# Two attention blocks in one kernel: its written-out instruction order is exchanged for another one

## The chip, the cores and the metric

The kernel runs on one core of one Trainium2 chip. A core has TensorE (PE, matmul), VectorE (DVE), ScalarE (ACT), GpSimd (POOL) and SyncE (SP); they run side by side and wait for one another by semaphores. Data moves between the device memory and the on-chip memory by 16 DMA engines, and transfers are issued by SP, POOL or ACT. The metric is the device time of the whole program in microseconds (us), median of several runs; lower is better. The profile is of one execution of its own.

## The reference

Two attention blocks, A and B, each with its own input and weights, S = 2048 rows, D = 640 columns, 32 heads of 20; their outputs stand side by side.

```python
def _A_ref(x, wqkv, wo):
    H = 32; Dh = D // H; W = 256
    q, k, v = split(x @ wqkv)                       # per head, [S, 20]
    scores = einsum("bhqd,bhkd->bhqk", q, k) * Dh ** -0.5
    scores = where((0 <= i - j) & (i - j < W), scores, -1e9)
    return merge(softmax(scores) @ v) @ wo

def _B_ref(x, wqkv, wo):
    q, k, v = split(x @ wqkv)
    phi = lambda t: where(t > 0, t + 1, exp(t)) + 1e-6
    kv = einsum("bhsd,bhse->bhde", phi(k), v);  z = sum_s phi(k)
    num = phi(q) @ kv;  den = phi(q) . z + 1e-6
    return merge(num / den) @ wo
```

A is softmax attention in a sliding window of 256 rows; B is linear attention, where the keys and values are summed once over all rows and then applied to every query.

## The kernel before

The two blocks are cut into 1,382 operations, numbered in the order in which the code makes them. Each is a closure that emits one or a few instructions on one engine: a chain of matmuls into one PSUM bank, an evacuation, a DMA. `Graph.op` notes what an operation reads and writes. No scheduler runs when the kernel is built. `Graph.run` replays a written-out string, `ORDER`, whose items are `number:engine`, for a matmul chain also the banks and how many of its matmuls are emitted here (`1264:P::1`), so that two chains can be interleaved. The order in which items stand on one engine is the order of that engine's queue[...]. `ORDER` was found by a search elsewhere; the `size=`, `count=`, `fix=` and `issue=` arguments of `dma(...)` only tell that search how long a transfer is, and emit nothing.

The work, with the lines of the profile:

- Block A's projections: queries and keys of eight groups of four heads (L433, five 128x512 matmuls each), values (L466, five 128x320). A tile has 32 rows for each of four heads, of which a head takes 20; the projection fills the other twelve with rows of the heads of groups 5, 6 and 7, which are carried to tiles of their own through device memory: relay writes `dqk<-QK` (L454), then three relay reads `QK<-dqk` (L461), 512 KB each, for groups 5, 6 and 7, once for each half of the rows.
- Scores, in 78 *units* of 512 columns, numbered 0 to 77: 16 to 32 small matmuls (L538) into the one four-bank PSUM tile U, then one exponential of all of it on ScalarE (L544, tile PT), then masks on VectorE (L573). Since there is one U, L538 of a unit waits for L544 of the unit before it. The units serve here as the clock of the order: "after unit 48" is a place in TensorE's queue.
- Probabilities times values (L644), per half of the rows and group of four heads, 16 operations in two parts each; the denominators go to memory and back three times (`RC<-ON`, `dr<-RD`, `RB<-dr`; L678, L680, L682), then a multiply (L689). Rows of groups 5 to 7 go back to the other groups' tiles through `do<-OS` (L692) and `OT<-do` or `QK<-do` (L698, L701). A's output projection is L710.
- Block B: keys (L746, with L737 to L739 for phi), their sums over the rows (L754, with the input loaded once more as XT, L752), z (L766), the product with the value weights (L796), that with the output weights (L810), then a small matrix to memory and back (L818 to L820). B's queries are L831, its denominators L838, its output again L710.

The loads that matter below, all issued by SyncE: B's value weights into the tile WV, 800 KB, L947, when A's values (L466) have all been made, for WV holds A's until then; B's query weights into WQ, 800 KB, L822, when A's last query chain (L433) is done; X tiles transposed on the way, five per 512 rows, 128 KB each (L391). At the start: four row blocks of A's input (L478), A's value weights in two halves (L876), A's query and key weights in pieces into R (L408).

Everything is in one program of about 8,900 TensorE instructions, a weight load and a matmul in turn. [...] they appear in the profile as DMA packets of kind "instruction".

Of the kernel before, what the change touches and what calls it, by code (L numbers as in the profile page):

```python
# [7 lines left out]
P = 128  # L8
# [7 lines left out]
2:G 10:S 0:A 4:S 5:P 6:A 7:S 8:P 9:A 11:P 12:A 17:S 54:P:0:5 58:P:1:2 13:S 55:A 14:P 15:A 58:P::3 1:S 32:D 31:A 28:S 62:P:2:5 71:P:3:3 72:P::2 73:A  # L16
66:P:0:5 63:D 59:D 16:S 68:P:2:3 69:P::2 67:A 23:S 52:P:1:1 56:P:3:5 52:P::4 29:S 64:P:0:5 70:A 22:S 37:D 120:P:2:3 121:P::2 27:S 26:S 57:A 122:A
176:P 60:P:3:5 30:S 74:P:2:3 65:D 75:P::2 53:A 77:P:0:3 35:D 18:S 61:D 177:A 25:S 39:D 94:P:1:4 84:P:3:5 19:S 33:A 76:D 78:P::2 24:S 36:D 21:S 20:S
34:A 94:P::1 95:D 41:S 575:S 180:P 82:P:2:3 80:P:1:5 82:P::2 79:D 149:G 44:S 179:D 96:P:0:3 181:A 81:D 86:P:1:2 97:P::2 98:D 86:P::3 83:D 183:P 3:G
85:A 99:P:3:3 111:P:0:3 87:A 184:A 100:P::2 102:P:1:1 185:D 49:S 92:P:2:3 42:S 101:A 38:A 186:P 187:A 92:P::2 93:D 105:P:3:3 106:P::1 102:P::1  # L20
106:P::1 102:P::1 46:S 43:S 90:P:2:1 103:P::2 90:P::3 147:S 104:D 107:A 189:P 182:D 112:P::2 88:P:3:5 45:S 407:P:1:5 150:G 148:G 113:D 108:P:0:1 188:D
90:P::1 108:P::1 190:A 89:A 204:P 408:A 178:D 91:D 108:P::1 144:S 51:S 191:D 409:D 410:D 48:S 411:P:3:1 146:G 109:P::1 411:P::1 109:P::1 123:P:2:3
411:P::3 110:D 399:P:1:5 205:A 207:P 124:P::1 132:P:0:1 124:P::1 132:P::2 412:A 133:P::2 50:S 40:D 400:A 208:A 413:D 401:D 402:D 586:S 155:G 414:D
403:P:1:5 211:P 125:A 47:S 134:D 404:A 192:P:30 405:D 212:A 209:D 795:S 406:D 206:D 152:G 135:P:2:3 136:P::2 419:P:1:5 467:S 153:G 137:D 210:D 420:A
421:D 422:D 215:P 216:A 427:P:2:1 193:P 195:D 427:P::3 154:G 213:D 194:D 423:P:1:5 145:G 214:D 464:S 427:P::1 117:P:0:1 428:A 196:G 466:S 231:P 429:D
117:P::2 463:S 114:P:3:3 217:D 115:P::2 118:P::2 151:S 430:D 424:A 425:D 443:P:2:5 218:D 232:A 119:A 116:D 234:D 161:S 426:D 235:P 233:D 160:G 157:G
219:P:30 138:P:1:3 139:P::2 444:A 445:D 446:D 459:P:2:5 197:D 236:A 140:A 237:D 238:P 415:P:1:1 220:P 415:P::4 465:S 460:A 461:D 239:A 416:A 462:D
221:D 222:D 435:P:2:5 417:D 241:P 439:P:3:5 126:P:0:1 418:D 431:P:1:5 198:G 158:S 436:A 437:D 438:D 451:P:2:5 223:G 240:D 242:A 244:P 432:A 433:D
434:D 126:P::2 127:P::2 485:P:1:5 440:A 468:S 199:G 452:A 469:S 453:D 454:D 477:P:2:5 201:S 441:D 442:D 243:D 200:G 245:A 129:P:3:2 259:P 129:P::1
202:G 128:A 472:S 471:S 130:P::2 141:P:0:3 224:D 225:G 478:A 479:D 470:S 480:D 486:A 142:P::2 487:D 447:P:2:5 131:D 488:D 260:A 162:S 163:S 143:A  # L30
262:P 246:D 172:S 455:P:3:5 493:P:1:5 448:A 156:G 203:D 263:A 169:S 164:G 166:G 226:S 449:D 450:D 229:G 456:A 247:P:02 227:G 266:P 170:G 265:D 457:D
458:D 481:P:3:5 494:A 495:D 496:D 473:P:1:5 228:S 167:G 264:D 267:A 270:P 537:S 261:D 540:S 268:D 482:A 483:D 484:D 248:P 269:D 497:P:3:5 474:A 475:D
271:A 159:S 476:D 501:P:1:1 286:P 249:D 273:D 501:P::4 171:S 272:D 230:D 250:A 274:P:02 498:A 287:A 499:D 502:A 539:S 290:P 291:A 251:G 500:D
513:P:3:5 503:D 173:S 541:S 538:S 504:D 289:D 489:P:1:5 490:A 252:D 253:S 293:P 275:P 491:D 492:D 505:P:1:5 514:A 294:A 515:D 516:D 529:P:3:5 276:D
277:D 296:P 569:P:0:4 561:P:2:5 174:S 569:P::1 165:G 506:A 507:D 530:A 508:D 531:D 532:D 546:S 517:P:1:5 297:A 295:D 573:P:3:5 299:P 570:A 278:S 562:D
518:A 300:A 519:D 565:P:2:5 520:D 566:A 547:P:0:3 548:P::2 549:A 665:P:1:2 279:D 256:G 288:D 314:P 665:P::1 254:S 292:D 315:A 666:P::2 301:D 298:D
255:S 667:A 257:G 574:D 544:S 258:D 521:P:2:5 542:S 668:P:0:3 280:S 669:P::2 522:A 168:G 317:P 318:A 670:D 523:D 524:D 302:P:31 553:P:0:3 543:S
554:P::2 319:D 533:P:2:5 555:A 545:S 321:P 534:A 535:D 536:D 686:P:0:3 282:S 687:P::2 320:D 303:P 304:D 567:P:2:5 283:G 568:D 322:A 325:P 323:D
509:P:3:5 671:P:2:3 672:P::2 316:D 324:D 305:A 688:A 326:A 328:D 677:P:1:2 342:P 281:G 510:A 674:P:0:3 673:A 284:G 511:D 285:D 327:D 306:S 175:S 343:A
556:P:2:3 557:P::2 558:A 675:P::2 677:P::1 512:D 346:P 329:P:32 307:D 308:S 312:G 347:A 344:D 309:S 678:P::2 676:D 550:P:0:3 717:G 679:D 551:P::2  # L40
311:S 310:S 552:A 348:D 349:P 706:G 350:A 680:P:1:3 681:P::2 576:P:0:4 682:D 330:P 331:A 332:D 351:D 352:P 353:A 525:P:1:5 703:G 577:P::4 578:P::4
563:P:3:5 701:G 354:D 355:P 333:G 526:A 356:A 732:S 527:D 528:D 1079:S 683:P:2:3 684:P::2 685:A 564:D 698:P:1:2 579:P::4 698:P::1 371:P 689:P:3:3
690:P::2 1080:S 345:D 313:D 739:S 699:P::2 357:D 704:G 719:S 580:A 718:G 372:A 358:P:20 374:P 334:D 702:S 335:S 700:A 1078:S 691:D 375:A 733:S
656:P:3:3 657:P::1 692:P:1:1 657:P::1 692:P::2 377:D 339:S 338:S 658:A 693:P::2 694:A 378:P 379:A 359:P 361:D 662:P:3:3 653:P:1:3 654:P::2 336:S
663:P::2 360:D 382:P 383:A 337:S 659:P:0:1 587:P:2:4 659:P::2 373:D 660:P::2 664:D 381:D 661:A 655:D 376:D 1082:S 581:P:3:4 340:D 384:D 385:D 362:S
738:S 828:P 829:A 380:D 582:P::4 363:D 583:P::4 584:P::4 722:G 386:P:10 585:D 831:D 832:P 588:P::4 833:A 712:G 571:P:3:3 589:P::4 590:P::4 591:D
571:P::2 714:G 721:S 836:P 572:D 734:S 387:P 707:S 837:A 649:P:2:3 647:P:3:5 649:P::2 713:G 389:D 650:D 341:S 709:G 388:A 637:P:0:5 648:D 639:P:1:5
716:G 840:P 364:S 643:P:2:2 559:P:3:1 643:P::1 559:P::1 643:P::1 559:P::2 640:D 643:P::1 559:P::1 839:D 638:A 644:D 711:G 597:S 736:S 598:P:0:1
603:P:1:4 598:P::3 834:D 841:A 843:P 735:S 710:S 599:P::4 604:P::4 600:P::4 844:A 835:D 605:P::4 1081:S 846:P 366:G 560:D 606:P::4 601:P::4 847:A
641:P:2:1 368:S 365:G 842:D 651:P:3:5 390:S 391:D 641:P::4 830:D 367:G 720:G 794:S 737:S 369:D 862:P 849:D 652:A 848:D 645:P:3:5 838:D 642:A 607:D  # L50
863:A 845:D 602:A 646:D 715:S 695:P:2:3 696:P::1 850:P:13 864:D 392:S 866:P 867:A 592:P:0:4 593:P::4 594:P::4 595:P::4 696:P::1 697:A 708:S 705:S
869:P 370:G 619:S 851:P 596:D 396:S 630:P:0 395:S 620:P:2:4 621:P::4 622:P::1 865:D 852:D 393:G 870:A 872:P 873:A 622:P::2 625:P:1:4 626:P::4 627:P::4
628:P::2 394:G 397:D 871:D 853:D 875:P 631:D 628:P::1 1194:S 874:D 622:P::1 876:A 878:D 608:S 628:P::1 398:S 724:G 629:D 623:P::4 609:P:3:4 610:P::4
624:A 611:P::1 868:D 891:P 611:P::1 614:P:0:4 854:G 855:D 615:P::4 892:A 611:P::2 877:D 612:P::4 613:A 729:S 793:S 616:P::2 894:P 895:A 616:P::2
617:P::4 749:G 879:P:21 632:P:3 745:S 633:D 748:S 747:S 740:G 742:S 618:A 746:S 897:P 799:P:0:10 796:P:3:10 797:P::10 750:G 744:G 880:P 800:D 893:D
751:G 898:A 900:P 901:A 741:S 743:G 759:P:0:4 798:D 882:D 754:P:3:2 856:G 759:P::1 754:P::1 811:P:1 754:P::1 881:D 812:A 760:D 817:P:2 754:P::1
823:P:0 824:A 792:S 904:P 905:A 805:P:1 726:G 857:G 807:P:0 755:D 818:D 815:P:3 1136:S 896:D 1083:P:2:3 1084:P::2 1085:A 920:P 921:A 806:D 903:D 902:D
821:P:1 822:A 808:D 816:D 634:S 899:D 752:P:0:5 858:S 1093:P:3:3 883:S 1086:D 1087:D 923:P 907:D 859:S 753:A 924:A 860:S 906:D 1094:P::2 1139:S 1095:A
861:D 884:D 803:P:2 908:P:10 804:D 813:P:2 814:D 926:P 927:A 1088:P:2:3 909:P 1089:P::2 1135:S 930:P 1137:S 1096:D 1097:D 635:S 1103:P:3:3 1104:P::2
1090:A 910:D 911:D 1098:P:1:1 925:D 819:P:0 756:S 1091:D 1092:D 931:A 1098:P::1 934:P 1105:A 757:P:2:5 820:D 1098:P::1 1145:P:0:1 1099:P::2 885:S  # L60
727:S 730:S 1145:P::2 636:D 1138:S 728:S 935:A 723:G 889:S 951:P 1106:D 1107:D 801:P:3 932:D 933:D 912:S 1100:A 1146:P::2 952:A 887:S 758:D 762:P:2:5
# [133 lines left out]
def kernel(  # L195
# [11 lines left out]
    _, S, D = A_x.shape  # L207
# [6 lines left out]
    HALF = D // 2  # L214
# [606 lines left out]
    def b_wq(key, earliest):  # L821
        dma("SP", lambda q: q.dma_start(out=WQB[:], in_=wB[:, :, 0:D]), key, w=WQK0, earliest=earliest, tag="wqB", size=2100, count=640, fix=2.6)  # L822
# [176 lines left out]
```

## Time and profile before

| what | us |
|---|---|
| median of 7 runs | 270.54 |
| lowest, highest | 267.76, 272.08 |
| profiled execution, device time | 270.1 |
| its span, first to last instruction | 268.4 |
| TensorE busy | 249.9 |
| ScalarE busy | 209.6 |
| VectorE busy | 170.8 |
| GpSimd busy | 62.1 |

The page gives for each engine its busy time and share of the span, then the span in 40 slices of 6.7 us: a digit is a busy share in tenths, PEclk the TensorE clock that was granted, DMA the share of the 16 DMA engines. TensorE's ends are modelled, so a busy slice is not necessarily a dense one. In a timeline, a row is a start, a length, an engine and line, the tiles, the shape and the count; in brackets stands the idle time before it and what ended it. "issue" there means that nothing the profile shows was waited for.

### The profile page before, as it was taken

The numbers are of one execution on the slowest core, as the hardware profiler recorded it, in microseconds if no ns is written. First come the engines' busy times: TensorE is split into PE (matmuls) and PEld (weight loads), VectorE is DVE, ScalarE is ACT, GpSimd is POOL, SyncE is SP. The second block draws the span as 40 slices with busy tenths as digits, with TensorE's granted clock in tenths as the row PEclk, the third lists the DMA queues.
The fourth block names the chain that finished last, engine by engine and source line by source line (L and its number), as shares of the span: only waits on it lengthen the run. The fifth ranks groups of instructions, "written<-read, shape, count | busy, mean of one in ns | idle before, by whom it ended". The sixth has DMA issues, their size and how long they took to land.

```text
span 268.4 us, 10336 instructions
## 1 busy us (share of the span) xinstructions
PE 249.9 (93%) x4439; PEld 147.6 (55%) x4439; DVE 170.8 (64%) x391; ACT 209.6 (78%) x233; POOL 62.1 (23%) x146
## 2 busy tenths in 40 slices
PE   7899999998899999999999969888988999999992
PEld 3555455555555545456666646545545555577771
DVE  0244578778977675474645323989879996846550
ACT  4558888999998988977687863999989999963211
POOL 5006301245120114304020702011301123045300
PEclk9999999999999999999999995999999999999998
DMA  7989895498988335558987893589899356255652
GB/s 193 238 167 231 158 187 81 91 130 175 167 131 150 94 101 129 104 146 202 167 231 162 253 188 70 106 154 137 194 221 207 93 155 208 86 150 167 209 195 101
DMA packets 69877, 42.47 MB, mean 158 GB/s; under 512 B 56010, under 2 KB 64906, under 8 KB 69818
## 3 DMA queue, kind: packets, MB, share of 16 engines
q1 hardware_dynamic: 63014, 33.25, 55.4%
q0 software_dynamic: 4192, 8.23, 14.2%
q8 instruction: 35, 0.57, 1.0%
q10 hardware_dynamic: 2624, 0.33, 0.8%
q14 instruction: 12, 0.10, 0.1%
HBM read 24.29 MB, written 10.59 MB: 130 GB/s over the span
## 4 chain that ended last, share of the span: by engine, by line
PE 63%; SPq 12%; DMA 8%; ACT 7%; DVE 5%; issue 4%; DVEq 0%; ACTq 0%
PE F L433 12%; PE F L710 10%; PE F L754 9%; SPq L391 8%; PE U L538 7%; PE F L746 5%; PE F L644 5%; PE U L710 5%; PE F L831 5%; ACT PT L544 4%; DMA RC<-ON 4%; PE F L466 3%; DMA QK<-dqk 2%; SPq L408 2%; DMA X<-in_B_x_dram 1%
## 5 line engine op out<-in xcount | busy, mean ns | idle before, releaser
L544 ACT ACTIVATE PT<-U 128x2048 bf16<-128x2048 f32 x78 | 146.7, 1881 | 21.7 <-PE U L538 18.5
L573 DVE TENSOR_TENSOR PT<-PT,MK 128x512 bf16<-128x512 bf16 (+2 forms) x116 | 46.8, 424 | 16.5 <-ACT PT L544 16.2
L538 PE MATMUL U<-QK 20*64 20x128 bf16 (+4 forms) x1600 | 33.3, 252 | 6.1 <-ACT PT L544 4.8
L538 PEld LDWEIGHTS <-QK 20*64 20x64 bf16 x1600 | 16.2, 103 | 28.0 <-issue 26.5
L682 POOL DMA_DIRECT2D RB<-dr x31 | 15.7, 509 | 56.8 <-DMA dr<-RD 29.5
L454 POOL DMA_DIRECT2D dqk<-QK x36 | 18.8, 526 | 43.3 <-ACT QK L344 19.8
L746 PE MATMUL F<-W,X 128*128 128x320 bf16 x160 | 26.7, 300 | 1.2 <-DVE R L739 0.9
L831 PE MATMUL F<-X,WQ 128*128 128x512 bf16 x100 | 27.2, 384 | 0.2 <-DVE G L348 0.2
L739 DVE SCALAR_TENSOR_TENSOR R<-F,E 128x320 bf16<-128x320 f32 (+1 forms) x47 | 25.9, 553 | 1.3
L737 ACT ACTIVATE E<-F 128x320 bf16<-128x320 f32 (+1 forms) x52 | 25.1, 503 | 1.8 <-PE F L746 1.3
L754 PE MATMUL F<-R,XT 128*128 128x320 bf16 x160 | 24.6, 300 | 0.0
L644 PEld LDWEIGHTS <-V 64*32 64x32 bf16 x1556 | 19.1, 93 | 8.7 <-issue 6.9
L644 PE MATMUL F<-PT,V 64*32 64x320 bf16 (+4 forms) x1452 | 23.3, 251 | 0.0
L746 PEld LDWEIGHTS <-X 128*128 128x128 bf16 x160 | 14.8, 98 | 10.2 <-issue 2.4
L466 PE MATMUL F<-WV,X 128*128 128x320 bf16 x120 | 19.0, 300 | 1.1 <-DMA WV<-in_A_wqkv_dram 1.1
L433 PE MATMUL F<-X,WQ 128*128 128x512 bf16 x75 | 19.9, 380 | 0.0
L348 DVE COPY ON<-F 128x512 f32<-128x512 f32 x24 | 16.0, 687 | 5.5 <-PE F L644 5.5
L433 PE MATMUL F<-X,WK 128*128 128x512 bf16 x75 | 19.2, 380 | 0.1
L754 PEld LDWEIGHTS <-XT 128*128 128x128 bf16 x160 | 14.8, 98 | 7.5 <-issue 1.0
L738 DVE TENSOR_SCALAR E<-E 128x320 bf16<-128x320 bf16 (+1 forms) x52 | 13.6, 261 | 6.7 <-ACT E L737 6.7
L344 ACT CAST QK<-F 128x512 bf16<-128x512 f32 x23 | 13.4, 588 | 4.2 <-PE F L433 4.1
L348 DVE CAST V<-F 128x320 bf16<-128x320 f32 x20 | 9.6, 490 | 10.8 <-PE F L466 10.8
(104 smaller groups left out, 320.4 us busy)
## 6 DMA issues: line engine op xcount, KB each, us to landing
RB<-dr SPq DMA_DIRECT2D x33, 128.0 KB
RB<-dr POOLq DMA_DIRECT2D x31, 128.0 KB, 3.9
QK<-dqk SPq DMA_DIRECT2D x6, 512.0 KB
XT<-in_B_x_dram SPq DMA_DIRECT2D x5, 512.0 KB
out_dram<-G SPq DMA_DIRECT2D x10, 160.0 KB
out_dram<-ST SPq DMA_DIRECT2D x8, 160.0 KB
do<-OS SPq DMA_DIRECT2D x4, 256.0 KB
WV<-in_A_wqkv_dram SPq DMA_DIRECT2D x2, 400.0 KB
```

The lines of the kernel that those rows point to most:

```text
L348: nc.vector.tensor_copy(out=dst, in_=src)
L433: mms.append((mm_t(NX), xread(slot, k) + [("wqk", i, m)], lambda ps, k=k: nc.tensor.matmul(ps[:], lhsT=WQK[i][:, k, m * P : (m + 1) * P], ...
L466: mms = [(mm_t(HALF), (xread(slot, k) if slot or kb > 3 else [("xb", kb)]) + [("wv", hf)], lambda ps, k=k, hf=hf: nc.tensor.matmul(ps[:, 0 ...
L538: nc.tensor.matmul(upper.at(1)[0][64 * rho : 64 * rho + 64, j, cc : cc + w], lhsT=QK[g][32 * j : 32 * j + Dh, kc : kc + 64], rhs=QK[g][32 ...
L544: nc.scalar.activation(out=pt, in_=upper.at(1)[0][:], func=ACT.Exp, scale=scale)
L573: nc.vector.tensor_tensor(out=p, in0=p, in1=mk, op=ALU.mult)
L644: nc.tensor.matmul(FB[box[rg]][32 * j : 32 * j + 32, qc : qc + w], lhsT=V[kb % NV][64 * rho : 64 * rho + 64, HV * h : HV * h + 32], rhs=PT ...
L710: mms = [(mm_t(HALF), [lkeys(c)] if not isinstance(lkeys(c), list) else lkeys(c), lambda ps, c=c, hf=hf: nc.tensor.matmul(ps[:, 0:HALF], l ...
L739: ({"DVE": dve_ps(n)}, lambda e, ps: nc.vector.scalar_tensor_tensor(out=dst, in0=ps[:, 0:n], scalar=1.0 + 1e-6, in1=e1, op0=ALU.add, op1=A ...
L746: mms = [(mm_t(HALF), [("x", slot, k), ("w1",)], lambda ps, k=k, b=b, hf=hf: nc.tensor.matmul(ps[:, 0:HALF], lhsT=X[slot][:, k, b * P : (b ...
L754: mms = [(mm_t(HALF), [("r1", tb), ("xt", c % 2)], lambda ps, tb=tb, c=c, hf=hf: nc.tensor.matmul(ps[:, 0:HALF], lhsT=XT[:, c % 2, tb, :], ...
L831: mms = [(mm_t(NX), [("x", slot, k)] + WQK0, lambda ps, k=k, c=c: nc.tensor.matmul(ps[:], lhsT=WQB[:, k, :].rearrange("p (f c) -> p c f", ...
```

## The change

`ORDER` is replaced as a whole. The graph, its operations and their dependences stay: the same matmuls, evacuations and transfers are emitted, 1,474 items before and 1,529 after, since some matmul chains are cut into more pieces. Which evacuation runs on VectorE or ScalarE, and which of the free DMAs SyncE or GpSimd issues, is part of the string and changes with it (SyncE 225 items before and 215 after, GpSimd 107 and 117). Besides it, six `size=` arguments change: of the X loads (540 to 481), A's row blocks (1700 to 1280), XT (430 to 380), WQ for B (2100 to 1800), A's value weights (900 to 640) and WV for B (1850 to 1550). All lines of the code below the string move down by 4.

The numbers of the operations that the text speaks of: 866, 869, 872, 875, 891, 894, 897, 900 are units 43 to 50, 926 is unit 54; 608 is the load of XT; 398 `do<-OS`; 729, 730, 731 the relay reads `QK<-dqk`; 793 the load of WV, 792 that of WQ; 740 to 751 the twelve reads `OT<-do`; 796, 797, 799 the product L796; 16 and 17 the two halves of A's value weights; 22 and 23 two pieces of R.

```diff
 ORDER = """
-2:G 10:S 0:A 4:S 5:P 6:A 7:S 8:P 9:A 11:P 12:A 17:S 54:P:0:5 58:P:1:2 13:S 55:A 14:P 15:A 58:P::3 1:S 32:D 31:A 28:S 62:P:2:5 71:P:3:3 72:P::2 73:A
...
-869:P 370:G 619:S 851:P 596:D 396:S 630:P:0 395:S 620:P:2:4 621:P::4 622:P::1 865:D 852:D 393:G 870:A 872:P 873:A 622:P::2 625:P:1:4 626:P::4 627:P::4
-628:P::2 394:G 397:D 871:D 853:D 875:P 631:D 628:P::1 1194:S 874:D 622:P::1 876:A 878:D 608:S 628:P::1 398:S 724:G 629:D 623:P::4 609:P:3:4 610:P::4
-624:A 611:P::1 868:D 891:P 611:P::1 614:P:0:4 854:G 855:D 615:P::4 892:A 611:P::2 877:D 612:P::4 613:A 729:S 793:S 616:P::2 894:P 895:A 616:P::2
-617:P::4 749:G 879:P:21 632:P:3 745:S 633:D 748:S 747:S 740:G 742:S 618:A 746:S 897:P 799:P:0:10 796:P:3:10 797:P::10 750:G 744:G 880:P 800:D 893:D
-751:G 898:A 900:P 901:A 741:S 743:G 759:P:0:4 798:D 882:D 754:P:3:2 856:G 759:P::1 754:P::1 811:P:1 754:P::1 881:D 812:A 760:D 817:P:2 754:P::1
...
+2:G 0:A 4:S 10:S 7:S 17:S 13:S 23:S 3:G 1:S 22:S 5:P 26:S 8:P 6:A 9:D 11:P 16:S 54:P:0:5 28:S 12:A 32:D 14:P 55:A 62:P:1:2 15:A 58:P:2:5 24:S 30:S
...
+559:P::2 593:P::4 1194:S 594:P::4 644:A 864:D 595:P::2 560:A 866:P 640:A 595:P::2 867:A 850:P:20 608:S 695:P:1:3 793:S 696:P::2 596:A 869:P 697:D
+620:P:3:4 870:A 397:D 625:P:1:4 626:P::3 621:P::1 851:P 398:S 729:S 872:P 853:A 852:D 792:S 621:P::3 873:A 725:S 865:D 626:P::1 622:P::1 854:G
+627:P::3 871:D 868:D 622:P::3 630:P:0 874:D 875:P 631:A 614:P:2:4 876:A 609:P:0:4 750:S 742:G 610:P::4 751:S 746:G 611:P::3 744:S 627:P::1 878:D 741:S
+747:G 891:P 877:D 623:P::2 740:S 892:A 748:G 628:P::1 615:P::4 724:S 726:G 628:P::1 616:P::4 628:P::2 623:P::2 893:D 629:A 611:P::1 612:P::1 894:P
...
-    dma("SP", lambda q: q.dma_start(out=WV[:], in_=wB[:, :, 2 * D : 3 * D]), 118, w=[("wv", 0), ("wv", 1)], tag="wvB", size=1850, count=640, fix=2.6)
+    dma("SP", lambda q: q.dma_start(out=WV[:], in_=wB[:, :, 2 * D : 3 * D]), 118, w=[("wv", 0), ("wv", 1)], tag="wvB", size=1550, count=640, fix=2.6)
```

## The prediction, made before the changed kernel was run

> **What bounds the kernel now.** I read the page's busy shares and slices first, then TensorE's waits, then the one stretch where they disagree, at single microseconds.
>
> ```profile
> PE 249.9 (93%) x4439; PEld 147.6 (55%) x4439; DVE 170.8 (64%) x391; ACT 209.6 (78%) x233; POOL 62.1 (23%) x146
> ...
> PEclk9999999999999999999999995999999999999998
> DMA  7989895498988335558987893589899356255652
> ...
> q8 instruction: 35, 0.57, 1.0%
> ```
>
> TensorE is the bound: 93% busy, against 78% for ScalarE. So only what stops or slows TensorE can move the span much, whatever else the order shuffles. One slice of the clock row stands at 5: full speed everywhere else, half speed in slice 25 (161 to 168 us). Just before it TensorE's timeline has its only long hole:
>
> ```profile
> 155.56 0.79 PE L644 MATMUL F<-PT,V 64*32 64x320 bf16 x60
> 156.27 0.73 PE L766 MATMUL F<-R,ones 128*32 128x320 bf16 x16
> 156.93 0.43 PE L538 MATMUL U<-QK 20*64 20x64 bf16 x24
> 157.29 1.18 PE L796 MATMUL F<-G,WV 128*120 128x120 bf16 x16
> 161.32 1.65 PE L796 MATMUL F<-G,WV 128*120 128x120 bf16 x14 [2.86 <-issue]
> 162.91 1.27 PE L644 MATMUL F<-PT,V 64*32 64x128 bf16 x52
> 164.10 0.65 PE L538 MATMUL U<-QK 20*64 20x192 bf16 x16
> 164.69 2.27 PE L710 MATMUL F<-W,OT 128*128 128x320 bf16 x8
> ```
>
> The hole (2.86 us) lies inside one L796 product: 16 matmuls went, 14 followed with the same operands. "issue" says no semaphore ended it. The clock is then half for some 6.6 us:
>
> ```profile
> 157.00:158.00 1.00, 1.00 (x36) 1.00 1.09 264
> 158.00:159.00 1.00, 0.47 (x6) 1.00 1.13 286
> 159.00:160.00 1.00, 0.00 (x0) 0.98 1.55 252
> 160.00:161.00 1.00, 0.00 (x0) 0.50 0.48 35
> 166.00:167.00 1.00, 1.00 (x6) 0.60 0.05 8
> 167.00:168.00 1.00, 1.00 (x29) 1.00 0.71 181
> ```
>
> (Columns: PE busy, granted clock, DMA share, GB/s.) The DMA engines were full up to 160. What filled them is in SyncE's issues:
>
> ```profile
> 146.88 1.29 SPq L461 DMA_DIRECT2D QK<-dqk  x1
> 148.22 0.43 SPq L947 DMA_DIRECT2D WV<-in_B_wqkv_dram  x1
> 149.34 2.48 SPq L698 DMA_DIRECT2D OT<-do  x6
> 151.91 0.40 SPq L822 DMA_DIRECT2D WQ<-in_B_wqkv_dram  x1
> ```
>
> That is 512 + 800 + about 250 + 800 KB in 5 us. The trace's packets show the rest. Queue 8 carries 35 packets of 16,384 bytes, TensorE's instructions. The twentieth starts at 158.82 and lands at 159.90, while the 1,280-byte packets of the WV and WQ loads run from 150.59 to 160.19; TensorE goes on at 161.32.
>
> How late was it? Counting loads and matmuls, undelayed fetches start when TensorE has passed three quarters of a 256-instruction block (at 191, 445 and 1,487 instructions; 0.75, 1.74, 5.81 blocks), and TensorE stopped dry at 5,313, which is 20.75. So each fetch has one block's issue time as cover. This one was due at instruction 5,057, passed at 154.3 us; it waited 4.5 us behind the loads, moved for 1.1, and took 1.4 to restart TensorE: 7.0 us against 4.0 of cover. Most other fetches waited 0 to 2.2 us. This block is among the thinnest in cover because L644, L766 and L538 issue many short matmuls.
>
> [...]
>
> **The change part by part.** The graph is the same: the same 4,439 matmuls and the same transfers. Only their order, PSUM banks and some engines differ, and six size constants that the order search, not the chip, reads (no cost).
>
> *The stall goes.* Before, SyncE issues XT, do<-OS, QK<-dqk, WV, the OT reads, WQ. After: XT, WV, do<-OS, QK<-dqk, WQ, one dqk write, the OT reads. WV's buffer is free once the last L466 is done (138.8 us), so WV can go right behind XT, near 142 on the old clock instead of 148.22: into a hole, for the 143:144 stretch moved 0 GB/s. WV is 800 KB, and 350 to 400 GB/s (the rate of 150 to 153 us) makes it 2.2 us less backlog when the fetch is due, again just after score unit 48: 4.5 - 2.2 = 2.3. By my PE sum the request also falls 0.8 us later (139.6 of work before unit 48 against 138.8): 1.5. Then 1.5 + 1.1 + 1.4 = 4.0 against 3.9 of cover, so a stall of 0.1; bounds 0 and 2.9, and I take 0.2. It saves 2.9 - 0.2 = 2.7.
>
> *The half clock goes with it.* Between 161 and 167, against the same shapes elsewhere: L796 x10 1.14 for 0.54, L644 x52 1.20 for 0.67, L538 0.59 for 0.36, eight L710 and their small neighbours 1.0 longer. Sum 2.4. After a hole of 0.2 I price it at nothing; if the clock falls, all 2.4 return. ScalarE cannot hide either sum: its exponential chain stood 5.5 us at this place, as each L544 needs the next L538.
>
> *What the moves cost.* OS and QK<-dqk now pass behind WV, so land up to 2.2 us later. Most OT rows had come by 157.9, the last by 159.6, and they are read at 164.7; QK's three heads are read from unit 58 (185 us). Both covers (5 us and more) suffice; without them it is 2.2 us. The read of the last QK third moves ahead, from about unit 62 to unit 54: before, unit 62 was held 0.9 us on QK<-dqk. I credit 0.5 (0 to 0.9).
>
> *The start.* Two R loads (480 KB) now precede the second WV half, at about 200 GB/s some 2.4 us; its first use stays near 12.8 us. The packets of that half ended at 9.27, so it would come at 11.7 [...]: cost 0.3 (0 to 1). The first score unit needs 7.8 us of PE work before it instead of 9.5. Worth nothing: TensorE is full from 10 to 60 us either way.
>
> *The rest.* Between score units I added TensorE's work and ScalarE's, each at this trace's durations (L538 0.36, L644 0.68, five 320-column matmuls 0.68, L544 1.88), and took the larger in each gap. Units 22 to 49: TensorE 73.2 before, 74.0 after (76.2 took place). Units 53 to 77: larger-of-two 63.8 and 63.8 (60.8 took place). After unit 77: 30.0 and 29.8. All PE work is the same, 233 us; switches between the kinds of matmul are 202 and 203. So nothing, within about 1.5 either way. A new order also brings unseen waits: 0.4 (0 to 3).
>
> *Sum*, from the profiled execution (270.1, that is 268.4 of span and 1.7 around it; 0.2% below the median 270.54): 270.1 - 2.7 - 2.4 - 0.5 + 0.3 + 0.4 = 265.2. Next in line is no single wait, but the ScalarE chain of units 53 to 77.
>
> **The rivals.** *The fetch is still late.* Nine of the twelve OT reads now come right ahead of it, and before they took from 152.7 to 157.9 with WQ. Then 2.7 + 2.4 return: 270.3. Against it: those reads are short of bytes, and 2.2 us of backlog are surely gone.
>
> *The stall moves later, slower.* The fetch due at unit 54 now has two 512 KB QK reads near it, four XB transposes and a store: by 2.5 us (148.80 to 151.32), 0.9 and 0.8 each, 9.4 us. SyncE's issues spread them over some 6, so 3 would be left; cover is 6.1, and 3 + 2.5 fits. Should one wait bunch them, 6.9 us of queue is the point from which hole and half clock outweigh the gain. At 8 us: 265.2 + (8 + 2.5 - 6.1) + 2.4 = 272.0.
>
> *Other waits eat half.* Denominator round trips or DVE's order in the ScalarE-bound part: 3 us, 268.2.
>
> *The search's order does not do it* is the first rival: whatever it assumed, only a packet that starts in time counts.
>
> **How the numbers follow.** Forecast, the stall gone: 0.68, range 262.5 to 267.6. Fetch still late: 0.14. Half eaten: 0.10. Stall later: 0.08. The range 262.5 to 269.8 leaves out most of the first and all of the last rival. One per cent, about what can be told from no change, is 2.7 us: under 267.8 lies the forecast with a share of the third case, 0.71; over 273.2 some of the last, 0.05; 0.24 between.
>
> **What would show it.** The clock row without the 5; no L796 hole marked "issue" over 1 us; WV issued before QK<-dqk near 142; L796 starting near 157; ends of both parts about 5 us earlier from unit 51 on. It is wrong if another hole of 2 to 3 us by "issue" stands elsewhere, most likely at units 54 to 57, or if ScalarE's L544 no longer keeps its 2.5 us pace.

## The result, and the profile after

The changed kernel takes 268.15 us (median of 27 runs, 264.27 to 272.85) against 270.56 for the kernel before beside it; the ratio is 0.9899, with an interval of 0.9873 to 0.9925. A second series of the same two kernels (e9 below) gave 266.04 against 269.62, ratio 0.9895 (0.9862 to 0.9929). So the change gains about 1.0%, 2.7 us: in the range, and half of the 5.3 us that were forecast. (The ratios leave out executions that lie over 1.5% above the fastest of their kernel; the medians are of all.)

The profiled execution of the changed kernel took 269.58 us, one of the longer ones; that of e9, the same kernel, 265.93. I read both, because what they share belongs to the order, and what they don't to one execution. First the page of the first, the lines that answer to those of before:

```profile
PE 252.1 (94%) x4439; PEld 147.5 (55%) x4439; DVE 171.2 (64%) x388; ACT 210.1 (78%) x236; POOL 68.3 (26%) x156
...
PEclk9999999999999999999999999999799999999998
DMA  7986952969958525394898969795877245353635
...
q8 instruction: 34, 0.56, 0.9%
```

The 5 in the clock row is gone from slice 25; a 7 has come in slice 29 (187 to 194 us). TensorE, at the place of the hole:

```profile
158.01 0.79 PE L648 MATMUL F<-PT,V 64*32 64x320 bf16 x60
158.73 0.73 PE L770 MATMUL F<-R,ones 128*32 128x320 bf16 x16
159.39 0.43 PE L542 MATMUL U<-QK 20*64 20x64 bf16 x24
159.75 1.53 PE L800 MATMUL F<-G,WV 128*120 128x120 bf16 x20
161.20 0.75 PE L648 MATMUL F<-PT,V 64*32 64x128 bf16 x52
```

No hole, the L800 product (L796 before) goes on at once, and the granted clock stays at 1.00 here; it falls at another place (columns: PE, PEld, DVE, ACT and POOL busy with counts, granted clock, DMA share, GB/s):

```profile
160.00:161.00 1.00, 1.00 (x18) 0.85 (x16) 0.38 (x2) 1.00 (x1) 0.04 (x1) 1.00 0.40 64
187.00:188.00 1.00, 0.77 (x18) 0.39 (x18) 0.75 (x3) 0.36 (x1) 0.74 (x2) 0.79 0.41 66
188.00:189.00 1.00, 1.00 (x3) 0.15 (x1) 1.00 (x3) 1.00 (x1) 0.73 (x2) 0.50 0.54 181
```

SyncE's issues in the changed kernel are in the order that the prediction named:

```profile
144.40 1.80 SPq L951 DMA_DIRECT2D WV<-in_B_wqkv_dram  x1
147.75 0.34 SPq L696 DMA_DIRECT2D do<-OS  x1
148.19 0.38 SPq L465 DMA_DIRECT2D QK<-dqk  x1
148.66 0.39 SPq L826 DMA_DIRECT2D WQ<-in_B_wqkv_dram  x1
...
152.56 1.94 SPq L702 DMA_DIRECT2D OT<-do  x5
```

By the packets, WV and WQ move from 147.13 to 156.61 us (150.59 to 160.19 before), the instruction fetch that had waited 4.5 us starts at 158.43 after 1.8 us of waiting and lands at 159.46, before TensorE needs it. In e9 it waited 0.55 us (154.18 to 154.73).

Where the time went, from the start of each unit's first score matmul and the end of the last matmul in the three traces:

| stretch, us | before | changed | changed (e9) | e9 less before |
|---|---|---|---|---|
| to unit 48 | 154.28 | 156.60 | 154.13 | -0.15 |
| unit 48 to 51 (the hole) | 13.41 | 9.17 | 7.83 | -5.58 |
| unit 51 to 58 | 17.39 | 17.57 | 17.57 | +0.18 |
| unit 58 to 60 | 4.95 | 7.99 | 8.14 | +3.19 |
| unit 60 to 64 | 10.63 | 9.85 | 9.86 | -0.77 |
| unit 64 to the last matmul | 63.01 | 62.86 | 62.85 | -0.16 |
| last matmul to the end of the span | 4.72 | 3.68 | 3.69 | -1.03 |

Two rows hold the case. The hole's stretch gained what was forecast for it, and seven units later the order gave more than half of that back: +3.0 and +3.2 us at units 58 to 60, in both executions. (The first execution lost besides 2.3 us at its start, and 1.2 us at L714 behind VectorE's `R`, L804, after unit 50; e9 did neither.) Two smaller rows are not the order's gain: in the profiles of e2, e3 and e8 below, which have the old order there, units 60 to 64 took 9.73 us and the last row 3.43 to 3.64, so the 10.63 and 4.72 of the kernel before belong to that one execution.

What stands at unit 58? VectorE, kernel before:

```profile
183.64 0.69 DVE L739 SCALAR_TENSOR_TENSOR R<-F,E 128x512 bf16<-128x512 f32 x1
184.25 0.34 DVE L679 RECIPROCAL RD<-RC 128x32 f32<-128x32 f32 x1
184.50 0.76 DVE L573 TENSOR_TENSOR PT<-PT,MK 128x256 bf16<-128x256 bf16 x3
185.18 1.22 DVE L689 TENSOR_TENSOR QK<-ON,RB 128x1024 bf16<-128x1024 f32 x1
```

and the changed kernel:

```profile
182.17 0.28 DVE L577 TENSOR_TENSOR PT<-PT,MK 128x256 bf16<-128x256 bf16 x1
184.25 0.35 DVE L683 RECIPROCAL RD<-RC 128x32 f32<-128x32 f32 x1 [1.81 <-DMA RC<-ON]
184.52 1.16 DVE L693 TENSOR_TENSOR QK<-ON,RB 128x1024 bf16<-128x1024 f32 x1
185.60 0.48 DVE L352 CAST G<-F 120x320 bf16<-120x320 f32 x1
```

TensorE behind it, in the changed kernel:

```profile
184.48 0.32 PE L648 MATMUL F<-PT,V 64*32 64x320 bf16 x4
186.13 0.80 PE L648 MATMUL F<-PT,V 64*32 64x256 bf16 x60 [1.34 <-DVE G L352]
...
189.16 1.27 PE L648 MATMUL F<-PT,V 64*32 64x128 bf16 x52
```

and in e9:

```profile
180.67 0.32 PE L648 MATMUL F<-PT,V 64*32 64x320 bf16 x4
182.72 1.18 PE L648 MATMUL F<-PT,V 64*32 64x256 bf16 x60 [1.73 <-DVE G L352]
```

The transfer that fetches the denominators, `RC<-ON` (from one on-chip tile to another; only the two after it pass through memory), was issued at 179.20 before and at 180.20 in the changed kernel:

```profile
179.20 1.62 SPq L678 DMA_DIRECT2D RC<-ON  x1
```

```profile
180.20 0.62 SPq L682 DMA_DIRECT2D RC<-ON  x1
```

Before, VectorE came to the reciprocal 5.05 us after the issue; in the new order it is ready for it after 2.25 (182.45). The view by tile gives no landing for this transfer. The counts of its semaphore in the trace do: they end 3.94 us after the issue before, 4.03 in the changed kernel, where the reciprocal starts 0.02 later. So the transfer took as long in both, and only the time that the order leaves it has changed. In e9 it took longer still, and the reciprocal started 4.72 us after the issue:

```profile
176.12 0.63 SPq L682 DMA_DIRECT2D RC<-ON  x1
180.84 0.35 DVE L683 RECIPROCAL RD<-RC 128x32 f32<-128x32 f32 x1 [2.20 <-DMA RC<-ON]
```

So VectorE stands, the multiply and the evacuation of G stand behind it in its queue, and L648 needs the PSUM bank that G frees. Then the clock is half for 3.4 us (187.58 to 190.99; in e9 182.84 to 186.25), as it had been for 6.8 us at the old hole (159.97 to 166.79).

### The profile page after: what moved, and what is told of

The parts are those of the page before. It is cut to its first block, busy times and chain, and to the rows that moved or that the text cites. A ratio compares the mean times of both kernels' runs of the same rounds, so it can differ in the third digit from the quotient of the medians.

```text
span 267.7 us, 10348 instructions
## 1 busy us (share of the span) xinstructions
PE 252.1 (94%) x4439; PEld 147.5 (55%) x4439; DVE 171.2 (64%) x388; ACT 210.1 (78%) x236; POOL 68.3 (26%) x156
## 4 chain that ended last, share of the span: by engine, by line
PE 80%; ACT 8%; issue 4%; DMA 4%; DVE 3%; SPq 0%; ACTq 0%; DVEq 0%
PE F L437 17%; PE F L714 10%; PE F L470 9%; PE F L758 9%; PE U L542 8%; PE F L750 7%; PE F L648 6%; PE F L835 6%; ACT PT L548 5%; PE U L714 5%; DMA WV<-in_A_wqkv_dram 2%; DMA RC<-ON 2%; ACT E L741 1%; DVE G L352 1%; DVE R L743 1%
## 5 line engine op out<-in xcount | busy, mean ns | idle before, releaser
L686 POOL DMA_DIRECT2D RB<-dr x35 | 17.6, 506 | 47.7 <-DMA dr<-RD 14.5
L835 PE MATMUL F<-X,WQ 128*128 128x512 bf16 x100 | 29.5, 394 | 0.2 <-DVE G L352 0.2
L542 PEld LDWEIGHTS <-QK 20*64 20x64 bf16 x1600 | 15.2, 103 | 25.7 <-issue 24.2
L458 POOL DMA_DIRECT2D dqk<-QK x29 | 15.2, 529 | 44.5 <-ACT WK L348 19.5
L758 PE MATMUL F<-R,XT 128*128 128x320 bf16 x160 | 25.9, 300 | 0.0
L648 PE MATMUL F<-PT,V 64*32 64x320 bf16 (+4 forms) x1452 | 23.9, 251 | 1.3 <-DVE G L352 1.3
L648 PEld LDWEIGHTS <-V 64*32 64x32 bf16 x1556 | 19.4, 93 | 10.2 <-issue 8.8
L470 PE MATMUL F<-WV,X 128*128 128x320 bf16 x120 | 23.7, 325 | 0.8 <-DMA WV<-in_A_wqkv_dram 0.8
L352 DVE CAST QK<-F 128x512 bf16<-128x512 f32 x20 | 13.6, 690 | 14.3 <-PE F L437 11.2
L437 PE MATMUL F<-X,WK 128*128 128x512 bf16 x75 | 20.9, 384 | 0.0
L437 PE MATMUL F<-X,WQ 128*128 128x512 bf16 x75 | 20.1, 380 | 0.0
L352 DVE COPY ON<-F 128x512 f32<-128x512 f32 x22 | 14.7, 688 | 8.4 <-PE F L648 8.3
L682 POOL DMA_DIRECT2D RC<-ON x11 | 8.1, 733 | 43.2 <-DVE E L742 13.5
```

Source lines behind the costliest of these rows:

```text
L352: nc.vector.tensor_copy(out=dst, in_=src)
L437: mms.append((mm_t(NX), xread(slot, k) + [("wqk", i, m)], lambda ps, k=k: nc.tensor.matmul(ps[:], lhsT=WQK[i][:, k, m * P : (m + 1) * P], ...
L470: mms = [(mm_t(HALF), (xread(slot, k) if slot or kb > 3 else [("xb", kb)]) + [("wv", hf)], lambda ps, k=k, hf=hf: nc.tensor.matmul(ps[:, 0 ...
L542: nc.tensor.matmul(upper.at(1)[0][64 * rho : 64 * rho + 64, j, cc : cc + w], lhsT=QK[g][32 * j : 32 * j + Dh, kc : kc + 64], rhs=QK[g][32 ...
L648: nc.tensor.matmul(FB[box[rg]][32 * j : 32 * j + 32, qc : qc + w], lhsT=V[kb % NV][64 * rho : 64 * rho + 64, HV * h : HV * h + 32], rhs=PT ...
L758: mms = [(mm_t(HALF), [("r1", tb), ("xt", c % 2)], lambda ps, tb=tb, c=c, hf=hf: nc.tensor.matmul(ps[:, 0:HALF], lhsT=XT[:, c % 2, tb, :], ...
```

## The experiments

All kernels below compute the whole reference. In short lists of items, "unit 10" means the place of that unit's scores in the string.

**e1 and e2: the start and the rest, each alone.** e1 takes the old order up to unit 10 and the new one from there; e2 the reverse. The beginning of e1's string, against the changed kernel's:

```diff
 ORDER = """
-2:G 0:A 4:S 10:S 7:S 17:S 13:S 23:S 3:G 1:S 22:S 5:P 26:S 8:P 6:A 9:D 11:P 16:S 54:P:0:5 28:S 12:A 32:D 14:P 55:A 62:P:1:2 15:A 58:P:2:5 24:S 30:S
+2:G 10:S 0:A 4:S 5:P 6:A 7:S 8:P 9:A 11:P 12:A 17:S 54:P:0:5 58:P:1:2 13:S 55:A 14:P 15:A 58:P::3 1:S 32:D 31:A 28:S 62:P:2:5 71:P:3:3 72:P::2 73:A
...
```

and of e2's, against that of before:

```diff
 ORDER = """
-2:G 10:S 0:A 4:S 5:P 6:A 7:S 8:P 9:A 11:P 12:A 17:S 54:P:0:5 58:P:1:2 13:S 55:A 14:P 15:A 58:P::3 1:S 32:D 31:A 28:S 62:P:2:5 71:P:3:3 72:P::2 73:A
+2:G 0:A 4:S 10:S 7:S 17:S 13:S 23:S 3:G 1:S 22:S 5:P 26:S 8:P 6:A 9:D 11:P 16:S 54:P:0:5 28:S 12:A 32:D 14:P 55:A 62:P:1:2 15:A 58:P:2:5 24:S 30:S
...
```

Expected of e1:

> The old order up to score unit 10, the new one from there on. First theory: the new order's start costs 2.5 us (in its profile every unit from 8 to 49 stands 2.5 us later than before, and TensorE's clock rises to full at 13.5 us and not at 6.4), so the old start gives 268.15 - 2.5 = 265.6. Rival: the late clock of that one profile is chance and happens to both starts alike; then 268.2, as the new kernel.

Expected of e2:

> The new order up to score unit 10, the old one from there on: the new start alone. First theory: 270.56 + 2.5 = 273. Rival (the start is worth nothing): 270.5.

Measured: e1 268.16 (17 runs; before 270.76), ratio 0.9930 (0.9891 to 0.9969); e2 270.23 (22 runs), ratio 1.0019 (0.9984 to 1.0054). The new start alone changes nothing that can be told, and putting the old one back gains nothing either. Both profiles have more to say. In e2, with the old order in the middle, the hole is there in its old place, and longer:

```profile
159.71 1.18 PE L795 MATMUL F<-G,WV 128*120 128x120 bf16 x16
164.91 1.65 PE L795 MATMUL F<-G,WV 128*120 128x120 bf16 x14 [4.02 <-issue]
```

In e1, besides a wait at the seam that the splice itself made (1.93 us on an X load at 57 us), unit 58 is held longest of all:

```profile
187.65 1.03 PE L648 MATMUL F<-PT,V 64*32 64x256 bf16 x60 [2.83 <-DVE G L352]
```

**e3: only the two loads, in the old order.** WV's load goes behind XT and WQ's behind the relay read in SyncE's queue; nothing else moves.

```diff
-628:P::2 394:G 397:D 871:D 853:D 875:P 631:D 628:P::1 1194:S 874:D 622:P::1 876:A 878:D 608:S 628:P::1 398:S 724:G 629:D 623:P::4 609:P:3:4 610:P::4
-624:A 611:P::1 868:D 891:P 611:P::1 614:P:0:4 854:G 855:D 615:P::4 892:A 611:P::2 877:D 612:P::4 613:A 729:S 793:S 616:P::2 894:P 895:A 616:P::2
...
+628:P::2 394:G 397:D 871:D 853:D 875:P 631:D 628:P::1 1194:S 874:D 622:P::1 876:A 878:D 608:S 793:S 628:P::1 398:S 724:G 629:D 623:P::4 609:P:3:4
+610:P::4 624:A 611:P::1 868:D 891:P 611:P::1 614:P:0:4 854:G 855:D 615:P::4 892:A 611:P::2 877:D 612:P::4 613:A 729:S 792:S 616:P::2 894:P 895:A
...
```

> The old order, but in SyncE's queue the WV load stands right behind the XT load and the WQ load right behind QK<-dqk, ahead of the OT reads, as in the new order; nothing else moves. First theory (the instruction fetch waits behind these loads, and hole and half clock are worth 5.3 us): the hole in L796 under 1 us, full clock there, 265.3. Rival: the gain needs the whole new order, the two loads alone leave the fetch late: 270.5.

Measured: 265.59 (6 runs, 264.32 to 267.36), ratio 0.9885 (0.9825 to 0.9945). Two moved items give as much as the whole change. They don't close the hole, as had been expected, they shorten it: the fetch waits 3.5 us instead of 4.5 (19 matmuls ahead of this place have no record in the trace, and are counted in),

```profile
158.24 1.18 PE L796 MATMUL F<-G,WV 128*120 128x120 bf16 x16
161.33 0.98 PE L796 MATMUL F<-G,WV 128*120 128x120 bf16 x14 [1.92 <-issue]
```

and the clock is half for 3.4 us (162.75 to 166.17) instead of 6.8. Unit 58 to 60 takes 4.95 us as in the kernel before, since VectorE's order is the old one.

**e4: the new order with the two loads put back.** WV behind the relay read, WQ behind the fifth `OT<-do`.

```diff
-559:P::2 593:P::4 1194:S 594:P::4 644:A 864:D 595:P::2 560:A 866:P 640:A 595:P::2 867:A 850:P:20 608:S 695:P:1:3 793:S 696:P::2 596:A 869:P 697:D
...
+559:P::2 593:P::4 1194:S 594:P::4 644:A 864:D 595:P::2 560:A 866:P 640:A 595:P::2 867:A 850:P:20 608:S 695:P:1:3 696:P::2 596:A 869:P 697:D 620:P:3:4
+870:A 397:D 625:P:1:4 626:P::3 621:P::1 851:P 398:S 729:S 793:S 872:P 853:A 852:D 621:P::3 873:A 725:S 865:D 626:P::1 622:P::1 854:G 627:P::3 871:D
...
+877:D 623:P::2 740:S 792:S 892:A 748:G 628:P::1 615:P::4 724:S 726:G 628:P::1 616:P::4 628:P::2 623:P::2 893:D 629:A 611:P::1 612:P::1 894:P 1135:S
...
```

> The new order, but the WV load moved back behind QK<-dqk and the WQ load behind the fifth OT read, as in the old order. First theory: the hole of about 3 us in L796 and the half clock after it return, 268.15 + 5 = 273. Rival: 268.2, the rest of the new order had made the fetch early enough.

Measured: 269.01 (14 runs), ratio 0.9982 (0.9937 to 1.0027). The gain is gone, as expected, but the kernel is not slower than before, as 273 would have been. A hole of the same kind is back, smaller:

```profile
160.18 1.12 PE L800 MATMUL F<-G,WV 128*120 128x120 bf16 x15
162.32 0.43 PE L800 MATMUL F<-G,WV 128*120 128x120 bf16 x5 [1.02 <-issue]
```

In this execution unit 48 started at 157.04 instead of 154.28, so the fetch was due later and waited 2.4 us (some 17 matmuls without a record counted in). e3 and e4 together show by their times that the place of the two loads is worth the gain, with either order around them. Their profiles show a part of it at this product: units 48 to 51 took 11.59 us in e3 against 13.41 before, and 9.02 in e4 against 7.83 in e9.

**e8: is it a matter of instruction blocks?** Old order, but the seven warm-up matmuls at the very start become 39 shorter ones, which makes every later TensorE instruction stand 64 places further on.

```diff
-    for _ in range(7):
-        nc.tensor.matmul(FB[0], lhsT=E1[0][:, 0:P], rhs=E1[0][:, 0:NX], start=True, stop=True)
+    for _ in range(39):
+        nc.tensor.matmul(FB[0][:, 0:92], lhsT=E1[0][:, 0:P], rhs=E1[0][:, 0:92], start=True, stop=True)
```

> The old kernel, but the 7 warm-up matmuls of 512 columns at the very start are 39 of 92 columns, so that all instructions behind them stand 64 places later. Theory (TensorE runs dry at the end of a block of 256 instructions whose successor is queued behind the loads): the hole moves 64 instructions back in the program, out of L796 and into L538 of unit 49, at about the same size, 2 to 4 us; the time is 270.6 plus about 1 for the longer warm-up. Rival (L796 itself waits for something, its operand or its bank): the hole stays inside L796.

Measured: 268.63 (20 runs; before 269.97), ratio 0.9946 (0.9910 to 0.9982), and in the profile:

```profile
157.49 0.23 PE L538 MATMUL U<-QK 20*64 20x64 bf16 x8
159.11 0.40 PE L538 MATMUL U<-QK 20*64 20x320 bf16 x16 [1.39 <-issue]
159.44 2.90 PE L796 MATMUL F<-G,WV 128*120 128x120 bf16 x30
```

The hole has left the L796 product, which is whole again, and stands 16 + 16 matmuls earlier, 64 instructions with their weight loads. In both kernels it is before TensorE's 5,314th instruction of the trace, and in e2 and e3 too, with the matmuls that have no record counted in, and in e4 within one instruction. No operand or wait moved with it; a boundary counted in instructions fits all five. In the kernel before, the first 34 fetches start 255 of TensorE's instructions apart in the mean (8,412 over 33 steps), so a block is about that long. The hole's size was not foreseen: 1.4 us and 3.4 us of half clock (160.09 to 163.50), and the kernel a little faster instead of slower.

**e5, e6, e7: the two places where the changed kernel's profile lost time.** e5 fills the start with four matmuls on zeros, to try whether the clock then comes up earlier (it came to full speed at 13.5 us in the changed kernel's profile, at 6.4 in that of before); e6 moves the evacuation of G ahead of the reciprocal on VectorE; e7 does both. e5, behind the transposes of the input:

```diff
+            for _ in range(2 if tb in (0, 2) else 0):
+                nc.tensor.matmul(FB[3], lhsT=E1[0][:, 0:P], rhs=E1[0][:, 0:NX], start=True, stop=True)
```

e6:

```diff
-1145:P::2 1101:D 952:A 1102:D 1146:P::2 937:D 1108:P:3 913:D 890:D 914:S 1109:A 955:P 758:A 762:P:3:5 804:D 956:A 761:G 938:P:10 763:D 915:G 916:S
+1145:P::2 1101:D 952:A 1102:D 1146:P::2 937:D 1108:P:3 804:D 913:D 890:D 914:S 1109:A 955:P 758:A 762:P:3:5 956:A 761:G 938:P:10 763:D 915:G 916:S
```

> The new kernel with two extra matmuls (zeros, 128x512, into a free bank) after the first and after the third row block of the start, where TensorE otherwise waits for a transfer. Theory: in three profiles with the new start TensorE's clock rose to full only at 13.5 to 13.7 us, in three with the old start at 5.7 to 10.4; with the gaps filled it rises near 6.5 to 10 us and the kernel gains 1.5 to 2.5 us: 266. Rival: the late clock at the start is made up later by slack, 268.2.

> The new kernel with one evacuation of the product with the output weights (G) moved on VectorE ahead of the reciprocal and the multiply after unit 57, behind which it stood. Theory: in the profiles with the new late part VectorE waits there for the denominators' transfer, and TensorE stands 1.2 to 3.1 us inside L648 for the bank that G holds; the clock then halves in two of them. Moved, the hole is gone and the kernel gains 1 to 3 us: 266. Rival: it is slack of the ScalarE chain and comes back by unit 64; 268.2.

> Both edits, the filled start and the evacuation moved. If both theories hold: 264 to 264.5. If neither: 268.2.

Measured, before 269.97: e5 265.78, ratio 0.9876 (0.9801 to 0.9951); e6 265.32, ratio 0.9853 (0.9785 to 0.9920); e7 265.05, ratio 0.9850 (0.9791 to 0.9910), six runs each. All lie near the 265 that had been forecast for the change, but the changed kernel was not among these runs, so the two were put side by side.

**e9 to e12: the same, with the changed kernel beside them.** e9 is the changed kernel, e10 is e5, e11 is e6, e12 is e7; the code is the same.

> The new kernel itself, beside its three variants on one chip. Theory (the missing part of the gain went to the late clock of the start and to the hold after unit 58): ratio to the old kernel 0.990, and slower than the three variants by 1 to 3 us; in its profile the clock rises at 13.5 us again and TensorE stands over 1 us inside the first L648 after unit 58. Rival (the three variants ran on a faster chip, and the edits do nothing): the same as they, within 0.7 us.

> The filled start a second time, beside the new kernel on one chip. Theory: 1 to 2.5 us under the new kernel, the clock up by 10 us at the latest. Rival: the same as the new kernel within 0.7 us.

> The moved evacuation a second time, beside the new kernel on one chip. Theory: 1 to 3 us under the new kernel, no hole inside L648 after unit 58. Rival: the same as the new kernel within 0.7 us, the hold being slack.

> Both edits a second time. Theory: 2.5 to 4 us under the new kernel, ratio to the old kernel 0.980 to 0.985, and the fastest of the four. Rival: within 0.7 us of the new kernel.

| kernel | median, us | runs | ratio to before (269.62) |
|---|---|---|---|
| e9, changed | 266.04 | 22 | 0.9895 (0.9862 to 0.9929) |
| e10, filled start | 265.88 | 22 | 0.9859 (0.9826 to 0.9893) |
| e11, G's evacuation ahead | 265.82 | 19 | 0.9896 (0.9861 to 0.9930) |
| e12, both | 264.80 | 6 | 0.9884 (0.9825 to 0.9944) |

No difference between the four stands out of the intervals, as the rival of each expectation had it. What a start with the clock up early and G's evacuation moved are worth is too small for these runs to tell (0.9 us either way for the larger sets), and the 2.6 us that were missing were not found by them. The filled start came to full clock at 4.1 to 6.2 us in its four profiles; but e9 did so at 5.4 without filling, so the late clock of the first profile belongs to that execution and not to the order.

e6's move is a different matter: the profiles show that it does only a part of what it was made for. VectorE no longer holds G, but it still stands at the reciprocal, and the next evacuation, of ST, is behind it. In e12 TensorE waits as long as before, for another tile,

```profile
183.00 0.30 PE L816 MATMUL F<-WK,R 120*120 120x320 bf16 x1 [1.53 <-DVE ST L352]
```

and in e6 for 1.14 us. In e11 there was no hold:

```profile
182.17 0.35 DVE L683 RECIPROCAL RD<-RC 128x32 f32<-128x32 f32 x1
```

There the transfer had been issued at 179.77 and had landed 2.4 us later, when VectorE had just got to the reciprocal. So this profile does not show that the move took the hold away: in e5, where nothing was moved on VectorE, the transfer was issued at 179.08, the reciprocal started 2.35 us later, and TensorE was not held either.

```profile
181.43 0.35 DVE L685 RECIPROCAL RD<-RC 128x32 f32<-128x32 f32 x1 [0.30 <-DMA RC<-ON]
```

e7 had no hold, and its transfer landed after 2.3 us. The execution of e11 had its half clock elsewhere (7.8 to 11.2 and 76.1 to 79.5 us) and ended with a longer span than e9, 264.8 against 264.1. The full exchange, with the reciprocal behind both evacuations, was not tried.

## Why the prediction was half right

*The hole goes (2.7 us), and its cause.* Right. The fetch waits 1.8 us, and 0.55 in e9, where 1.5 was estimated; there is no stall where 0.1 to 0.2 was; WV was issued first, at 144.40 on a clock that ran 2.3 us late, and at 141.93 in e9 (142 was named). e8 shows the cause by instruction count, e3 and e4 the loads as what delays the fetch. In five profiles TensorE stood at this one boundary for 1.0 to 4.0 us (before 2.86, e2 4.02, e3 1.92, e4 1.02, e8 1.39).

*The half clock goes with it (2.4 us).* Right at its place: units 48 to 51 gained 5.58 us in e9, where 2.7 + 2.4 were forecast. Wrong for the kernel, and the term that was missed by most. This step said "after a hole of 0.2 I price it at nothing", an estimate from the one hole of one profile, and looked for no other hole, while 3.4 us of half clock came back behind the next one. How little half clock went away can be read from the mean clock listed for each run, by which its time is 2 x (1 - clock) x span where the clock is full or half (0.9824 of 268.39 us in the profile of before gives 9.4; its trace has 6.8 us at 0.50 in the middle and 2.6 at the end): in the runs that the ratios use, a mean of 4.9 us before (70 runs) and 3.4 after (29), in which up to 2.6 us of idle tail is counted; over all executions, 6.5 (129) and 6.0 (50). So the change took away 0.6 to 1.5 us of half clock per run, not the 6.8 of the profile; at the forecast's own rate (2.4 for 6.8) that is worth 0.2 to 0.5. A straight line of span against half-clock time through all these executions gives 265.0 us before and 263.2 after where there is no half clock: by this estimate the change gains 1.8 us apart from the clock, where the other terms of the sum made 2.5.

*What the moves cost; the last third of QK (0.5).* The cost is right: OS and QK behind WV held nobody. The gain is not shown: units 60 to 64 took 0.77 us less than in the kernel before, but e2, e3 and e8 have the old order there and took 9.73, less than the changed kernel. The wait of 0.9 us that was credited stood in one of four profiles.

*The start (0.3 lost).* An estimate: the second half of A's value weights had its last packet at 11.19 where 11.7 was reckoned, and what this cost was not shown. e2's ratio, 1.0019 (0.9984 to 1.0054), agrees with it, and as well with nothing.

*The rest: ±1.5, and unseen waits 0.4 (0 to 3).* This is the other step that failed. Its sum per gap compared TensorE's work with ScalarE's and left VectorE out, and the one wait that decided was on VectorE: the new order puts the reciprocal 2.25 us behind the issue of its transfer, where the old one left 5.05. In the two profiles it cost 3.0 and 3.2 us, the end of the range: 1.65 and 2.05 us from the start of the four L648 matmuls to that of the next sixty, and a half clock of 3.4 us, which in the first profile cost 1.4 against e11's full speed (1.44 for 0.84, 1.27 for 0.74 and 0.90 for 0.63 in three groups). It could have been read off before: the transfer took 3.94 us in the kernel before, and the two strings show what VectorE has between. With 2.25 us for it, VectorE's wait comes to 1.7; 1.81 was measured.

*The rivals.* "Other waits eat half: denominator round trips or VectorE's order, 3 us, 268.2" had a tenth of the chance, and it is what both profiles show, at the time that was measured (268.15); that the time agrees so closely is luck, for the second series of the same kernel had 266.04. "The fetch is still late" and "the stall moves to units 54 to 57" fell: in the nine traces that have the new order with its loads in place, the longest wait by "issue" from 150 to 200 us is 0.49 us (e7). The queue of 6.9 us from which that stall would outweigh the gain comes to 6.5 by the sum beside it (265.2 + 6.5 + 2.5 - 6.1 + 2.4 = 270.5); nothing hangs on it.

*What stays open.* In five profiles with the loads in place and VectorE's order of the change (the first, e9, e1, e5, e10), units 58 to 60 took 5.1 to 9.4 us, 8.0 in the mean, against 4.95 with the old order: again 3.0, half clock included. That this makes up what is missing of the median is not shown, for no kernel here has the hold surely taken out: e6 and e12 removed half of the reason only, and in e7 and e11 the transfer landed early. The hold's size changes from one execution to another with the transfer: with VectorE's order of the change, TensorE stood 0 us in e5 and 0.87 in e4, where the reciprocal started 2.35 and 2.65 us after the issue, and 1.34 in the first, 1.73 in e9, 2.13 in e10 and 2.83 in e1, where it started 4.05 to 4.72 us after it. Why the transfer takes 2.3 us in one execution and 4.7 in another was not found. Nor does the half clock depend on these two holes alone: in e5, e6 and e11 it also came at 74.4 to 76.1 us.

## What to carry to other kernels

When an order is exchanged as a whole, the hole that it removes is the smaller half of the work: walk every engine's queue at the same places, and for each instruction that waits for a DMA, compare the time from issue to need in both orders with the landing time that the trace shows. Large loads can also delay a long program's instruction fetches: here a fetch waited 4.5 us behind two loads of 800 KB, two load issues moved into a quiet stretch gave as much as the whole change, and counting TensorE's instructions told where the fetch was due. A saving sized on one execution with a clock dip in it should not be counted in full, since the dip can come back behind another hole: here 2.4 us were forecast for it, and the runs' clocks account for 0.2 to 0.5.

## What the runs showed of the hardware that was not expected

- A hole of about 1 us can be followed by the half clock, and needn't be. All ten traces with the new order in the middle have the same two holes at unit 20, 0.60 to 0.62 and 1.03 to 1.04 us, the second ending 1.5 us after the first; in e5, e6 and e11 the clock fell right there (74.4, 74.8 and 76.1 us), in the other seven it did not. In e6:

```profile
72.47 0.43 PE L542 MATMUL U<-QK 20*64 20x128 bf16 x24 [0.60 <-ACT PT L548]
73.93 2.01 PE L750 MATMUL F<-W,X 128*128 128x320 bf16 x10 [1.03 <-DVE R L743]
```

  The same two rows stand in e9 with 1.52 for 2.01, at full clock. A half clock then lasted 3.4 us, or 6.8 in e2, e10 and the profile of before. So the term "half clock" of a forecast is a chance and not a length; what decides it was not found.
- The clock first reached full speed between 4.1 and 13.7 us after the start, with the same instructions at 5.4 and at 13.5.
- The same hole with the same order at the same place had 2.86 us (before) and 4.02 (e2).
- A transfer of 128 pieces of 128 bytes between two on-chip tiles, always at the same place of the order, landed 2.3 us after its issue in e7 and 4.7 in e9.
